# A small weight piece on 24 partitions in 3 steps instead of 16 partitions in 4

## The chip, the cores and the metric

One core of a Trainium2 chip runs the kernel. The metric is device time in microseconds (us) of one execution; lower is better.

## The reference

A decode step for two rows x of width 448: a layer norm, then attention with a cached K and V (16 query heads on 8 kv heads, 4096 positions, head size 256) through w_q and w_o, times the SiLU of a bilinear feed-forward block (width 1792), added to x.

```python
xn = _layernorm(x)                          # x: [2, 1, 448]
q = (xn @ wq).reshape(B, Sq, 16, 256).transpose(0, 2, 1, 3)
p = _softmax(einsum("bhqd,bhkd->bhqk", q, k) * 256 ** -0.5)
s = einsum("bhqk,bhkd->bhqd", p, v).transpose(0, 2, 1, 3).reshape(B, Sq, 4096) @ wo
g = _silu(((xn @ w_gate) * (xn @ w_up)) @ w_down)
return x + s * g
```

All values are float32. K and V alone are 2 x 64 MB; with the weights some 158 MB have to be read once.

## The kernel before

The work is cut into 16 steps i, one for each pair of kv head and batch row. Step i takes K of its pair as k{i} [128, 8192] and V as v{i} [128, 8192]. `scores(i)` (L247) multiplies q with K into PSUM and finds a maximum, `softmax(i)` (L260 to L271) takes the exponential and turns it, `values(i)` (L286) multiplies with V. The main loop runs values(i), then scores(i+1), then softmax(i+1). In between come, after steps 0, 2, 4 and 8, the feed-forward block (`ffn_in`, `ffn_out`), the second half of the queries (`query(1)`) and the first part of the product with w_o (`project`). After the loop comes a tail: scores and values of step 15, the rest of w_o (`project`, and `project_last` at L329, whose weights, wo2, come with the last V), and two VectorE operations and the store (L398 to L400).

What is loaded, and in which order, stands in the list `todo` (filled by `plan`, sent by `issue`). SP issues all loads of K, V and weights into one queue: wq0 (the first half of w_q, at L76), a small piece wqx at L80, k0 (`first`), then `vk` pieces that hold v{i} and k{i+1} together (128 rows of 64 KB), with the other weights between them: wgu, wdq and wo after vk pieces 0, 2 and 8. At the end come last0 (k15 and v14) and last1 (v15 and wo2), the latter in cuts of 4096, 3072, 1024, 1344, 1344, 448, 224 and 224 columns. The K and V buffers are a ring of two, the weights share one slot: SP issues a load when the buffer is free, that is when the reads of its former contents on PE are done. The first four loads wait for nothing.

`query(h)` calls `rows`, which multiplies the 448 rows of w_q's half h with the transposed, normed x. 384 rows are three blocks of 128 (L175). The last 64 rows do not fill 128 partitions. For the second half, and for the feed-forward weights, they are folded: columns of the left half on partitions 0 to 63, of the right half on 64 to 127 (L188). For the first half, wq0 keeps only one of the four column blocks c in folded form on each half (L184, c = 2 and 3); the rows for c = 0 and 1 lie in wqx. It lies on `SIDE` = 16 partitions of 16 KB each: 4 steps times 2 column blocks times 512 columns. Step j of `NK` = 4 multiplies rows 384+16j to 384+16j+15 (L181), once for each column block. The matching pieces of x, xeT, are made by four transposes (L139) and a copy (L140). xeT borrows the start of the tile oT1, which has no other use until the end.

On the host, wqx is built as an array of `SIDE // 4` groups of 5 rows, of which the load reads the first 4: the fifth row is padding that keeps the groups apart in the access pattern. The load is

```python
nc.sync.dma_start(loaded["wqx"][:SIDE], wqx[:, :4])      # L80
```

so 16 partitions on one side stand against 4 groups of 4 rows on the other.

Of the kernel before, what the change touches and what calls it, by code (L numbers as in the profile page):

```python
# [13 lines left out]
B, D = 2, 448  # L14
# [3 lines left out]
W = 32  # L18
DUP = W // 2
NK = 4  # L20
# [6 lines left out]
LATE = 24  # L27
THIRD = [24, 25, 26, 28, 29, 30, 31, 27]
PART = 14 * (D + 512)
SIDE = 16  # L30
EXTRA = 8
EPS = 1e-5


# [5 lines left out]
def gated_decode_block(ctx: ExitStack, tc: tile.TileContext, x, first, vk, last0, last1, wq0, wqx, wdq, wo, wgu, out):  # L40
    nc = tc.nc
# [11 lines left out]
    def bank(name=None):  # L53
        return psum.tile([128, 512], F32, name=name, bufs=1) if name else two()[:, 0]
# [8 lines left out]
    def issue(n=1):  # L63
        for names, src, cuts in todo[:n]:
# [12 lines left out]
            if names == ["wq0"]:  # L77
                at = src.shape[1]
                loaded["wqx"] = t[:, at:at + EXTRA * 512]
                nc.sync.dma_start(loaded["wqx"][:SIDE], wqx[:, :4])  # L80
        del todo[:n]
# [22 lines left out]
    ident = const.tile([128, 128], F32)  # L104
# [18 lines left out]
    xn = e1[:, 1]  # L123
    nc.vector.tensor_scalar(xn[:, :D], xc, rstd, None, op0=OP.mult)
    nc.vector.tensor_scalar(xn[:, D:], xc[:, 384:], rstd, None, op0=OP.mult)
    pt = bank()
# [5 lines left out]


    oT1 = const.tile([128, 3, 2, REP, W], F32)
    xeT = oT1[:SIDE].rearrange("p g d r m -> p (g d r) m")[:, :NK]
    pt = bank()
    for j in range(NK):
        at = 384 + j * SIDE
        nc.tensor.transpose(pt[:SIDE, B * j:B * (j + 1)], xn[:, at:at + SIDE], ident[:B, :B])  # L139
    nc.vector.tensor_copy(xeT.rearrange("p k (b j) -> p k b j", b=B),  # L140
                          pt[:SIDE, :NK * B].rearrange("p (k b) -> p k b", b=B)[:, :, :, None].to_broadcast([SIDE, NK, B, DUP]))

    both = work.tile([128, D], F32, name="h")[:B, :W].rearrange("p (b j) -> p b j", b=B)
    nc.vector.tensor_copy(both, ident[:B, :B, None].to_broadcast([B, B, DUP]))
    pt = bank()
    for c in range(NT):
        nc.tensor.matmul(pt[W * c:W * (c + 1), :SL], both.rearrange("p b j -> p (b j)"), x2[:, c * SL:(c + 1) * SL],
                         start=True, stop=True)
# [18 lines left out]
    def rows(ps, w, n, extra=None):  # L167


        def block(i):  # L170
            return w[:, i * n:(i + 1) * n]

        for k in range(3):
            for c in range(NT):
                nc.tensor.matmul(ps[W * c:W * (c + 1), :n], xnT[:, k, :], block(NT * k + c), start=k == 0, stop=False)  # L175
        if extra is not None:

            for j in range(NK):
                for c in range(2):
                    at = (c * NK + j) * n  # L180
                    nc.tensor.matmul(ps[W * c:W * (c + 1), :n], xeT[:, j, :], extra[:SIDE, at:at + n], start=False, stop=j == NK - 1)  # L181
                    if j == 0:
                        half = slice(64 * c, 64 * (c + 1))
                        nc.tensor.matmul(ps[W * (2 + c):W * (3 + c), :n], xnT[half, 3, :], block(12)[half], start=False, stop=True)  # L184
            return
        for c in range(NT):
            half = slice(0, 64) if c < 2 else slice(64, 128)
            nc.tensor.matmul(ps[W * c:W * (c + 1), :n], xnT[half, 3, :], block(12 + c % 2)[half], start=False, stop=True)  # L188
# [4 lines left out]
    def query(h):  # L193
        ps = bank()
        rows(ps, loaded[f"wq{h}"], 512, None if h else loaded["wqx"])
        for r in range(REP):
            nc.vector.transpose(qT[h][:, :, :, :, r, :].rearrange("p b g d j -> p (g d) b j"),  # L197
                                ps[:, r * 256:(r + 1) * 256])
# [16 lines left out]
    def ffn_in():  # L215
        pp = two()
        for i, w in enumerate(("wg", "wu")):
            rows(pp[:, i], loaded[w], FC)
        g = work.tile([128, FC], F32, name="h")
        nc.scalar.copy(g, pp[:, 0, :FC])  # L220
        h = work.tile([128, FC], F32, name="h")
        nc.vector.tensor_mul(h, pp[:, 1, :FC], g)
        nc.vector.transpose(hT.rearrange("p i m -> p (i m)"), h)
# [34 lines left out]
    def softmax(i, s, m, pT=None):  # L258
        sm = bank("sm")
        nc.tensor.transpose(sm[:1, :128], m[:, 0:1], ident)  # L260
        mx = work.tile([1, NT, W], F32, name="mx", bufs=1)
        nc.vector.tensor_reduce(  # L262
            mx, sm[:1, None, :128].rearrange("p o (c j) -> p o j c", c=NT).to_broadcast([1, NT, W, NT]),
            axis=AX.X, op=OP.max)
        nc.tensor.transpose(sm[:, 128:129], mx.rearrange("p c j -> p (c j)"), one)  # L265
        nc.vector.tensor_scalar(m[:, 1:2], sm[:, 128:129], -1.0 / 16, None, op0=OP.mult)  # L266
        p = work.tile([128, 2, 512], F32, name="p", bufs=1)
        nc.scalar.activation(p, s, AF.Exp, bias=m[:, 1:2], scale=1.0 / 16, accum_out=su[:, place(i):place(i) + 1])  # L268
        if pT is None:
            pT = work.tile([128, 2, 512], F32, name="pT", bufs=1)  # L270
        nc.vector.transpose(pT.rearrange("p h n -> p (h n)"), p.rearrange("p h n -> p (h n)"))  # L271
        return pT
# [66 lines left out]
    p = softmax(0, *ss)  # L339
    for i in range(LAST):  # L340
        g, b = divmod(i, B)
# [9 lines left out]
        p = softmax(i + 1, *ss)  # L351
# [19 lines left out]
    ps = [p]  # L371
# [4 lines left out]
    p = softmax(LAST + 1, *ss, last[:, :1024].rearrange("p (h n) -> p h n", h=2))  # L376
# [75 lines left out]
```

## Time and profile before

| | us |
|---|---|
| median of 3 runs | 376.22 |
| lowest, highest | 376.15, 376.42 |
| the profiled execution | 376.37 |
| its span in the profile | 374.6 |

The span runs from the first to the last instruction of the profile; the 1.8 us beside it are outside of what the profile shows. In the profile, PE is TensorE (PEld its weight loads), DVE is VectorE, ACT ScalarE, SP SyncE, which issues the loads. "L286" is line 286 of the kernel. A chain row gives start, duration and what ran or was waited for. PE does each float32 matmul of 512 columns as two passes, so counts of PE rows are twice those of the code. DMA queue q1 holds the loads that SP issues; q8 and q14, of kind "instruction", are reads of program code.

### The profile page before, as it was taken

How to read it: one execution, taken by the hardware profiler on the slowest of the kernel's cores; microseconds unless marked ns; L12 is line 12 of the kernel's file. 1: busy time of each engine (PE TensorE's matmuls, PEld its weight loads, DVE VectorE, ACT ScalarE, POOL GpSimd, SP SyncE). 2: the span in 40 equal slices, each digit the busy share in tenths (PEclk: the TensorE clock that was granted, in tenths of full speed). 3: DMA queues.
4: the chain of work that ended last, by engine and by line, in shares of the span. 5: the costliest groups of instructions: out<-in, count | busy, mean ns of one | idle time of the engine just before them, and what ended most of it. 6: DMA issues, size and time to landing. Idle time of an engine off the chain costs nothing.

```text
span 374.6 us, 3200 instructions
## 1 busy us (share of the span) xinstructions
PE 203.6 (54%) x1446; PEld 57.3 (15%) x1446; DVE 72.6 (19%) x121; ACT 25.3 (7%) x39; POOL 1.2 (0%) x7
## 2 busy tenths in 40 slices
PE   1796458082734090857372665721819180909785
PEld 0111112020211020212020111200202020202222
DVE  4002130104040003040404041300120312040541
ACT  1000010001020002010101010100010101010120
POOL 1000000000000000000000000000000000000000
PEclk9956598768578577696768596885867687776999
DMA  8999899999999999999999999999999999999994
GB/s 327 432 500 441 374 432 448 448 436 435 419 442 441 441 441 400 422 448 450 420 441 434 443 415 409 457 441 434 450 420 422 441 434 427 436 409 441 413 416 178
DMA packets 4356, 158.78 MB, mean 424 GB/s; under 512 B 614, under 2 KB 1000, under 8 KB 1384
## 3 DMA queue, kind: packets, MB, share of 16 engines
q1 hardware_dynamic: 4340, 158.59, 98.2%
q8 instruction: 11, 0.18, 0.2%
q14 instruction: 1, 0.01, 0.0%
q10 hardware_dynamic: 4, 0.00, 0.0%
HBM read 158.54 MB, written 0.06 MB: 423 GB/s over the span
## 4 chain that ended last, share of the span: by engine, by line
DMA 74%; PE 24%; issue 1%; SPq 0%; DVE 0%
DMA ring<-vk 66%; PE o L286 11%; PE s L247 8%; DMA ring<-last 5%; DMA slot<-wq 3%; PE s L181 2%; PE s L175 1%; PE s L184 1%; PE s L329 0%; SPq L76 0%; PE sm L279 0%; DVE h L398 0%; DVE h L399 0%
## 5 line engine op out<-in xcount | busy, mean ns | idle before, releaser
L286 PE MATMUL o<-ring,pT 128*32 128x512 f32 x480 | 87.3, 893 | 112.4 <-DMA ring<-vk 112.4
L248 DVE TENSOR_REDUCE m<-s 128x1 f32<-128x1024 f32 x16 | 19.6, 1222 | 221.9 <-PE s L247 221.9
L247 PE MATMUL s<-ring,qT 128*32 128x512 f32 x512 | 60.7, 616 | 0.9 <-PE s L181 0.9
L286 PEld LDWEIGHTS o<-ring,pT 128*32 128x32 f32 x480 | 21.7, 155 | 167.8 <-issue 154.2
L268 ACT ACTIVATE p<-s,m 128x1024 f32<-128x1024 f32 x16 | 17.8, 1113 | 293.7 <-DVE m L266 293.7
L247 PEld LDWEIGHTS s<-ring,qT 128*32 128x32 f32 x512 | 17.5, 114 | 42.3 <-issue 39.7
L271 DVE STREAM_TRANSPOSE pT<-p 128x1024 f32<-128x1024 f32 x15 | 18.7, 1245 | 21.2 <-ACT p L268 21.2
L175 PE MATMUL s<-slot,xnT 128*32 128x512 f32 (+1 forms) x96 | 14.1, 733 | 7.3 <-DMA slot<-wq 4.3
L260 PE MATMUL sm<-ident,m 128*1 128x128 f32 x16 | 4.3, 270 | 18.8 <-DVE m L248 18.8
L265 PE MATMUL sm<-one,mx 1*128 1x1 f32 x16 | 3.5, 220 | 14.6 <-DVE mx L262 14.6
L262 DVE TENSOR_REDUCE mx<-sm 1x128 f32<-1x512 f32 x16 | 10.7, 670 | 2.1 <-PE sm L260 2.1
L347 DVE COPY ob<-o 128x512 f32<-128x512 f32 x14 | 9.5, 681 | 0.0
L181 PE MATMUL s<-slot,oT 16*32 16x512 f32 x16 | 7.4, 942 | 0.0
L320 PE MATMUL wide<-slot,oT 128*32 128x448 f32 x48 | 6.6, 699 | 0.6 <-DVE oT L312 0.6
L229 PE MATMUL s<-slot,hT 128*32 128x448 f32 x28 | 4.7, 786 | 3.4 <-DMA slot<-wdq 3.4
L260 PEld LDWEIGHTS sm<-ident,m 128*1 128x1 f32 x16 | 1.3, 79 | 33.0 <-DVE m L248 32.4
L175 PEld LDWEIGHTS s<-slot,xnT 128*32 128x32 f32 x96 | 3.6, 134 | 15.2 <-issue 15.2
L295 PE MATMUL cb<-ob,add_blocks 128*32 128x64 f32 (+2 forms) x64 | 4.3, 384 | 2.4 <-DVE ob L347 1.6
L197 DVE STREAM_TRANSPOSE qT<-s 128x256 f32<-128x256 f32 x4 | 1.6, 428 | 19.4 <-PE s L181 18.4
L265 PEld LDWEIGHTS sm<-one,mx 1*128 1x128 f32 x16 | 2.2, 136 | 17.6 <-DVE mx L262 17.6
L268 ACT ACT_TABLE_LOAD x2 | 2.6, 1283 | 27.4 <-DVE m L266 25.2
L286 PE MATMUL wide<-ring,slot 128*32 128x512 f32 x32 | 4.1, 597 | 0.0
(68 smaller groups left out, 46.8 us busy)
## 6 DMA issues: line engine op xcount, KB each, us to landing
ring<-last SPq DMA_DIRECT2D x2, 4096.0 KB, 24.1
slot<-wdq SPq DMA_DIRECT2D x1, 6720.0 KB
slot<-wgu SPq DMA_DIRECT2D x1, 6272.0 KB, 30.6
slot<-wo SPq DMA_DIRECT2D x1, 5376.0 KB, 41.9
ring<-first SPq DMA_DIRECT2D x1, 4096.0 KB, 21.0
slot<-wq SPq DMA_DIRECT2D x1, 3328.0 KB, 10.7
ring<-last SPq DMA_DIRECT2D x1, 2048.0 KB, 14.1
ring<-last SPq DMA_DIRECT2D x1, 1536.0 KB
```

The source lines that it names most:

```text
L175: nc.tensor.matmul(ps[W * c:W * (c + 1), :n], xnT[:, k, :], block(NT * k + c), start=k == 0, stop=False)
L181: nc.tensor.matmul(ps[W * c:W * (c + 1), :n], xeT[:, j, :], extra[:SIDE, at:at + n], start=False, stop=j == NK - 1)
L247: nc.tensor.matmul(s[W * c:W * (c + 1), h, :], q[:, d], k[:, h, d, c, :], start=d == 0, stop=d == 1)
L248: nc.vector.tensor_reduce(m[:, 0:1], s, axis=AX.XY, op=OP.max)
L260: nc.tensor.transpose(sm[:1, :128], m[:, 0:1], ident)
L262: nc.vector.tensor_reduce(mx, sm[:1, None, :128].rearrange("p o (c j) -> p o j c", c=NT).to_broadcast([1, NT, W, NT]), axis=AX.X, op=OP.max)
L265: nc.tensor.transpose(sm[:, 128:129], mx.rearrange("p c j -> p (c j)"), one)
L268: nc.scalar.activation(p, s, AF.Exp, bias=m[:, 1:2], scale=1.0 / 16, accum_out=su[:, place(i):place(i) + 1])
L271: nc.vector.transpose(pT.rearrange("p h n -> p (h n)"), p.rearrange("p h n -> p (h n)"))
L286: nc.tensor.matmul(o[W * t:W * (t + 1), :], pT[:, h, at:at + 2 * W:2], loaded[f"v{i}"][:, e * 512:(e + 1) * 512], start=e < NT, stop=e >= ...
L320: nc.tensor.matmul(wide[W * t:W * (t + 1), :D], heads(oT, i, first), loaded["wo"][:, i * D:(i + 1) * D], start=i < NT, stop=i >= LATE - NT)
L347: nc.vector.tensor_copy(ob[:, place(i) % 8], o)
```

## The change

wqx is laid on 24 partitions instead of 16, in 3 steps of 24, 24 and 16 rows instead of 4 steps of 16, each partition holding 12 KB instead of 16 KB. The load reads 6 groups of 4 rows instead of 4 groups of 4. The last 8 partitions of the third step are zeros, which are loaded but not used. In all wqx grows from 256 KB to 288 KB. Three transposes instead of four make xeT, two copies instead of one move it (24 and 16 partitions), and the multiplication takes 6 matmuls instead of 8. Nothing else of the program changes, nor the order of the loads.

```diff
-SIDE = 16
-EXTRA = 8
+SIDE = 24
+NS = 3
+EXTRA = 2 * NS
...
-    for j in range(NK):
-        at = 384 + j * SIDE
-        nc.tensor.transpose(pt[:SIDE, B * j:B * (j + 1)], xn[:, at:at + SIDE], ident[:B, :B])
-    nc.vector.tensor_copy(xeT.rearrange("p k (b j) -> p k b j", b=B),
-                          pt[:SIDE, :NK * B].rearrange("p (k b) -> p k b", b=B)[:, :, :, None].to_broadcast([SIDE, NK, B, DUP]))
+    for j in range(NS):
+        lo, hi = 384 + j * SIDE, min(384 + (j + 1) * SIDE, D)
+        nc.tensor.transpose(pt[:hi - lo, B * j:B * (j + 1)], xn[:, lo:hi], ident[:B, :B])
+    for n, lo, hi in ((SIDE, 0, NS - 1), (64 - SIDE * (NS - 1), NS - 1, NS)):
+        nc.vector.tensor_copy(xeT[:n, lo:hi].rearrange("p k (b j) -> p k b j", b=B),
+                              pt[:n, lo * B:hi * B].rearrange("p (k b) -> p k b", b=B)[:, :, :, None].to_broadcast([n, hi - lo, B, DUP]))
...
-            for j in range(NK):
+            for j in range(NS):
+                n_rows = min(SIDE, 64 - j * SIDE)
                 for c in range(2):
-                    at = (c * NK + j) * n
-                    nc.tensor.matmul(ps[W * c:W * (c + 1), :n], xeT[:, j, :], extra[:SIDE, at:at + n], start=False, stop=j == NK - 1)
+                    at = (c * NS + j) * n
+                    nc.tensor.matmul(ps[W * c:W * (c + 1), :n], xeT[:n_rows, j, :], extra[:n_rows, at:at + n],
+                                     start=False, stop=j == NS - 1)
...
     wqx = np.zeros((SIDE // 4, 5, EXTRA * 512), np.float32)
-    ends = wq0[:64, 12 * 512:].reshape(NK, SIDE // 4, 4, 2, 512).transpose(1, 2, 3, 0, 4)
+    ends = np.zeros((NS * SIDE, 2, 512), np.float32)
+    ends[:64] = wq0[:64, 12 * 512:].reshape(64, 2, 512)
+    ends = ends.reshape(NS, SIDE // 4, 4, 2, 512).transpose(1, 2, 3, 0, 4)
```

More of the change, by code (lines that the diff above doesn't have):

```diff
@@ L134, in gated_decode_block @@
     oT1 = const.tile([128, 3, 2, REP, W], F32)
-    xeT = oT1[:SIDE].rearrange("p g d r m -> p (g d r) m")[:, :NK]
+    xeT = oT1[:SIDE].rearrange("p g d r m -> p (g d r) m")[:, :NS]
     pt = bank()
-    for j in range(NK):
-        at = 384 + j * SIDE
-        nc.tensor.transpose(pt[:SIDE, B * j:B * (j + 1)], xn[:, at:at + SIDE], ident[:B, :B])
-    nc.vector.tensor_copy(xeT.rearrange("p k (b j) -> p k b j", b=B),
-                          pt[:SIDE, :NK * B].rearrange("p (k b) -> p k b", b=B)[:, :, :, None].to_broadcast([SIDE, NK, B, DUP]))
+    for j in range(NS):
[4 more added lines that the diff above has]
+                              pt[:n, lo * B:hi * B].rearrange("p (k b) -> p k b", b=B)[:, :, :, None].to_broadcast([n, hi - lo, B, DUP]))
     both = work.tile([128, D], F32, name="h")[:B, :W].rearrange("p (b j) -> p b j", b=B)
```

## The prediction

> **What bounds the kernel now.** I read the page from the top: engines, then the DMA lines, then the queues.
>
> ```profile
> PE 203.6 (54%) x1446; PEld 57.3 (15%) x1446; DVE 72.6 (19%) x121; ACT 25.3 (7%) x39; POOL 1.2 (0%) x7
> ...
> DMA  8999899999999999999999999999999999999994
> ...
> DMA packets 4356, 158.78 MB, mean 424 GB/s; under 512 B 614, under 2 KB 1000, under 8 KB 1384
> ## 3 DMA queue, kind: packets, MB, share of 16 engines
> q1 hardware_dynamic: 4340, 158.59, 98.2%
> q8 instruction: 11, 0.18, 0.2%
> q14 instruction: 1, 0.01, 0.0%
> ```
>
> The loads (q1) keep 16 DMA engines busy 98.2% of the span; PE, the busiest compute engine, 54%. So the time is set by bytes, and more exactly by the DMA engine that is through last. The next view is the chain that ended last, in order of time (start, us, what).
>
> ```profile
> 0.74 10.70 DMA slot<-wq
> 11.44 0.14 issue
> 11.57 4.91 PE s L175 x24
> ...
> 21.23 5.28 PE s L181 x12
> 26.51 0.91 issue
> 27.42 6.41 PE s L247 x32
> 33.83 0.02 issue
> 33.84 42.61 DMA ring<-vk
> ...
> 307.95 29.68 DMA ring<-vk
> 337.63 0.14 issue
> 337.77 6.50 PE o L286 x32
> ...
> 349.55 20.43 DMA ring<-last
> 369.98 0.14 issue
> 370.12 1.45 PE s L329 x48
> ```
>
> From 33.84 on, each stage starts with a landing. Two landings matter: the last vk piece, seen at 337.63 (307.95+29.68), which starts the tail of PE work, and a piece of wo2 seen at 369.98, for which L329 sits idle before its second part:
>
> ```profile
> PE s L329 <- DMA ring<-last: 0.5, 1, 0.5
> ```
>
> **How wqx sits on the DMA engines.** SP issues all that it can, then waits: two rows of its timeline, one of its waits.
>
> ```profile
> 1.18 0.78 SPq L80 DMA_DIRECT2D slot<-wqx  x1
> 2.47 0.50 SPq L76 DMA_DIRECT2D ring<-vk  x1
> ```
>
> ```profile
> SPq L76 <- DMA slot<-wqx: 10.4, 1, 10.4
> ```
>
> SP was free at 2.47+0.50=2.97 and saw wqx land 10.4 later, at 13.4: 1.9 after wq (11.44), though wqx is only 256 KB behind wq's 3328 KB. The DMA view of short windows says why. A DMA closes with a 4-byte packet on each engine that it used. The windows 10.1 to 11.2, 11.2 to 13.1, 19.8 to 20.9 and 22.4 to 22.8, one row each:
>
> ```profile
> DMA packets 37, 0.55 MB, mean 501 GB/s; under 512 B 16, under 2 KB 16, under 8 KB 16
> ```
>
> ```profile
> DMA packets 37, 0.95 MB, mean 500 GB/s; under 512 B 4, under 2 KB 4, under 8 KB 4
> ```
>
> ```profile
> DMA packets 28, 0.92 MB, mean 834 GB/s; under 512 B 12, under 2 KB 12, under 8 KB 12
> ```
>
> ```profile
> DMA packets 16, 0.79 MB, mean 1966 GB/s; under 512 B 4, under 2 KB 4, under 8 KB 4
> ```
>
> "Under 512 B" counts the closing packets: wq closes on 16 engines, wqx on 4; k0 then closes on 12 engines first and on 4 about 2.4 us later. Wqx lies on four engines, which stay behind: SP queues the next DMAs early, so no engine ever waits for the others.
>
> The trace's packet records (which no view lists one by one) let each engine's queue be followed, since a packet starts 4 ns before the one ahead of it ends. I did that for all 16, from wq to the end. A 16 KB packet takes 611 ns, a 12 KB one (the piece 4096 to 7168 of last1) 460, a 64 KB one 2418. Closing packet of the last vk piece, and of wo2's last piece, us:
>
> ```
> engines                           last vk piece     wo2, last piece
> 4, nothing extra                  333.9 to 334.2    367.46 to 367.80
> 6, one q8 fetch                   335.3 to 336.1    368.96 to 369.65
> 2, two q8 fetches                 336.5 and 335.7*  370.10 and 370.24
> 3, wqx                            336.28 to 336.51  369.85 to 370.07
> 1, wqx and the one q14 packet     337.30            370.86
> (* its second fetch came later, at 355.8)
> ```
>
> Two windows confirm the last row: 336.6 to 337.4, then 370.3 to 370.9.
>
> ```profile
> DMA packets 9, 0.26 MB, mean 328 GB/s; under 512 B 1, under 2 KB 1, under 8 KB 1
> ```
>
> ```profile
> DMA packets 16, 0.01 MB, mean 21 GB/s; under 512 B 2, under 2 KB 16, under 8 KB 16
> ```
>
> One engine alone closes the last vk piece; one alone still works from 370.3 on (two closing packets, 21 GB/s; a busy engine's share of 424 is 26.5). It is a wqx engine that was also held up 0.8 us by the q14 packet at 145.1. **The kernel ends when that engine does**, plus what PE does after.
>
> **The change, part by part.**
>
> *The load.* Before: 4 engines x 4 rows x 16 KB. After: 24 partitions against 6 outer groups, so by the same pattern (16 partitions against 4 groups gave 4) 6 engines x 4 rows x 12 KB. Packets start 4 ns early, so a wqx engine carried 4 x (611-4) = 2.43 us and will carry 4 x (460-4) = 1.82: **0.60 us less on each of the four old engines**, the late one among them. Check from the page's mean: 16 KB less on an engine at 26.5 GB/s is 0.62. Two more engines each get 1.82 us that they did not have.
>
> How the engines are chosen, no row names. The Trainium skill ("DMA: Bandwidth & Descriptors", "Why a DMA increments its semaphore by 16 and not by 1") says that a DMA runs on the largest number up to 16 that divides both sides' slowest dimension, and on the lowest-numbered engines; the four closing packets of wqx agree with the number, and by it the new pair would be the fifth and sixth engine.
>
> *Where the 0.60 goes.* Late engine: last vk piece 337.30 to 336.70; next is the two-fetch engine, 336.53, so the whole 0.60 counts. At the end: 370.86 to 370.26; next the other two-fetch engine, 370.24. Again 0.60, and no more than 0.62. If the new pair had nothing extra, they reach 334.2+1.82=336.1 and 367.8+1.82=369.6, below both: no cost.
>
> *The tail of PE.* Chain 337.77 to 369.65 is PE, DVE and ACT work. It starts 0.60 earlier, but the granted clock is half there at first (windows of 3 us; PEclk is third from the end):
>
> ```profile
> 338.00:341.00 3.00, 3.00 (x16) 0.68 (x12) 0.00 (x0) 0.00 (x0) 0.00 (x0) 0.50 0.91 393
> 341.00:344.00 3.00, 3.00 (x20) 0.81 (x16) 0.00 (x0) 0.00 (x0) 0.00 (x0) 0.57 1.09 470
> 344.00:347.00 3.00, 3.00 (x32) 0.94 (x28) 0.00 (x0) 0.00 (x0) 0.00 (x0) 1.00 0.94 404
> ```
>
> If the clock rises at the same moment as before, 0.60 us of half-speed work is worth 0.30. Then PE is ready for L329's second part 0.30 to 0.60 before 369.65, at 369.05 to 369.35. The wo2 piece would be seen 0.60 before 369.98, at 369.38, plus the 0.14 issue: 369.52. So it is still DMA that starts it, and the 0.60 survives. If PE gained nothing at all, it would start at 369.65: 0.47 of 0.60 is kept.
>
> *PE at the start.* L181 has 6 matmuls instead of 8, L139 3 transposes instead of 4.
>
> ```profile
> L181 PE MATMUL s<-slot,oT 16*32 16x512 f32 x16 | 7.4, 942 | 0.0
> L139 PE MATMUL s<-ident,pT 2*16 2x2 f32 x4 | 0.2, 159 | 0.0
> L140 DVE COPY oT<-s 16x128 f32<-16x128 f32 x1 | 0.3, 270 | 0.0
> ```
>
> The 16 rows are 8 matmuls of two passes, paced about 0.47 a pass by 7.4/16. Four passes fewer save 4 x 0.47 = 1.9 us before scores(0). It is worth nothing: vk0 is not there yet, and the timeline has L286 waiting for it (in brackets):
>
> ```profile
> 26.53 0.34 SPq L76 DMA_DIRECT2D slot<-wgu  x1
> ...
> 42.46 3.59 PE L286 MATMUL o<-ring,pT 128*32 128x512 f32 x13 [6.07 <-DMA ring<-vk]
> ```
>
> The 1.9 us only lengthens that 6.07. SP's next DMA (wgu, behind L181) goes out at about 24.6 instead of 26.53; by the packet records vk0 keeps the engines busy to 39.2 at least, so nothing gains. The DVE copy becomes two, +0.27 us, while PE waits for wq until 11.57: hidden; without that cover 0.27 us. No wait is added: PE and SP wait for wqx at the same two places. Between 0 and 1.9 for PE's early part I take 0, since a DMA wait of 6.07 stands behind it.
>
> Sum: **-0.60 us**. Profiled execution: 376.37-0.60=375.77. It ran 0.15 above the median, so against the median 376.22-0.60 = **375.62**, -0.16%. A measurement tells about 0.2% (0.75 us) from no change.
>
> **The rivals.**
>
> 1. *The new pair already carries instruction fetches (slower).* In time order the first eight q8 fetches go to eight different engines, the ninth, tenth and eleventh to the first three again: a ring of eight. None was on a wqx engine; four others had none. So the two new engines come from twelve, of which eight are in the ring. With one fetch, 335.3 to 336.1 plus 1.82 gives 337.1 to 337.9 against 337.30, and 368.96 to 369.65 plus 1.82 gives 370.8 to 371.5 against 370.86: -0.1 to +0.6 us (376.1 to 376.8). With two, 336.53+1.82=338.35 or 370.24+1.82=372.06: +1.05 to +1.2 (377.3 to 377.4). It decides from the point where a new engine's own extra exceeds 337.30-334.2-1.82 = 1.3 us, about one fetch. For it: eight of twelve. Against: the sixteen fall into eight engines of the ring and eight others, and all four of wqx are among the others; if those eight are one block that wqx fills from one end, the next two are in it too. A ring in the middle would not leave them free.
>
> 2. *Bytes count, not the busiest engine.* The load grows by 32 KB; at the mean of 424 GB/s that is +0.08 us: 376.3. The Trainium skill (same page, "Anatomy of one DMA") fits a DMA issued from GpSimd as a fixed time plus its bytes over one rate, which by its 436 GB/s would also be an estimate of +0.08. Against it: the closing packets of k0, four of them 2.4 us late, and one engine alone at the end.
>
> 3. *No gain, another end.* Start-up differs between executions, so two-fetch engines or PE's tail can be last before the late engine is: 0 to -0.3 us, 375.9 to 376.2.
>
> 4. *The DMA does not run on six.* On three engines, 8 rows each, 8 x 0.456 = 3.65 instead of 2.43: +1.2 (377.4); on two, 12 rows, +3.0 (379.3). On sixteen it cannot be even: 24 rows over 16. Against: the four of before.
>
> **How the numbers follow.** Forecast 0.56 (375.4 to 375.9), rival 1 0.28 (0.19 with one fetch, 0.09 with two), rival 2 0.03, rival 3 0.08, rival 4 0.05. The range 375.3 to 376.9 holds the forecast, rivals 2 and 3 and the one-fetch part: 0.86 less their edges. Two fetches and rival 4 are left out. Faster by over 0.2% needs under 375.47, the lower edge of the forecast: 0.10. Slower needs over 376.97: two fetches, rival 4 and a little of one fetch: 0.17. Same: 0.73.
>
> **What would show it.** The window that holds wqx's end has 6 closing packets, earlier (wqx seen near 12.8 instead of 13.4); k0 closes on 10 engines, then on 6 about 1.8 us later; the last vk piece is seen near 337.0, L329's second part starts near 369.5, the span is about 374.0. L181 shows 12 passes. Wrong if k0's late group is not six, if the last vk piece is seen at 337.5 or later (rival 1), or if it is seen earlier and L329 is not (PE's tail).

## The result, and the profile after

The changed kernel takes 376.47 us (median of 19 runs, 376.23 to 377.84), the kernel before 376.26 (19 runs, 376.15 to 376.68): ratio 1.0013, 95% interval 1.0007 to 1.0019. It is a little slower, where 0.60 us less was forecast. The times fall into two clusters: 13 runs from 376.23 to 376.77 (median 376.45), and 6 from 377.53 to 377.84. The kernel before has only one; none of its 69 runs beside the experiments is above 377.13. That 376.47 lies within the 375.3 to 376.9 of the prediction is owed to the rivals for which the range was widened, not to the forecast.

The profiled execution (376.46, span 374.7) is of the lower cluster. The page's DMA lines:

```profile
DMA packets 4366, 158.82 MB, mean 424 GB/s; under 512 B 616, under 2 KB 1002, under 8 KB 1386
## 3 DMA queue, kind: packets, MB, share of 16 engines
q1 hardware_dynamic: 4350, 158.62, 98.2%
q8 instruction: 11, 0.18, 0.2%
q14 instruction: 1, 0.01, 0.0%
```

The load is 10 packets more than before: two more engines, 4 rows and a closing packet each. The share of q1 is what it was. The chain that ended last:

```profile
307.72 29.97 DMA ring<-vk
337.69 0.14 issue
337.83 6.17 PE o L290 x32
...
349.28 20.77 DMA ring<-last
370.06 0.14 issue
370.19 1.09 PE s L333 x40
```

The last vk piece is seen at 337.69 (337.63 before), the wo2 piece at 370.06 (369.98 before). Nothing of the 0.60 us has arrived at either place, and the sign that the prediction named for its first rival, the last vk piece seen at 337.5 or later, is there. PE's early part did become shorter. First the rows of L184, then from the timeline SP's issue of wgu and the first values:

```profile
L184 PE MATMUL s<-slot,oT 24*32 24x512 f32 x8 | 3.1, 600 | 0.0
L184 PE MATMUL s<-slot,oT 16*32 16x512 f32 x4 | 1.0, 588 | 0.0
```

```profile
22.07 0.33 SPq L77 DMA_DIRECT2D slot<-wgu  x1
...
42.24 3.64 PE L290 MATMUL o<-ring,pT 128*32 128x512 f32 x16 [10.09 <-DMA ring<-vk]
```

Twelve passes instead of 16, and wgu goes out at 22.07 instead of 26.53, more than the 1.9 us foreseen, because L184's passes also took a mean of 600 ns or less instead of 942. From 20 to 22 us PE's granted clock was 0.50 before and is 1.00 now: most of these passes now run before the clock falls. It ends as a longer wait for vk0, 10.09 us instead of 6.07: worth nothing, as forecast.

The closing packets of k0, in the windows 20.0 to 21.1 and 21.6 to 22.5, and those of the last vk piece in 336.95 to 337.4:

```profile
DMA packets 26, 0.85 MB, mean 775 GB/s; under 512 B 10, under 2 KB 10, under 8 KB 10
```

```profile
DMA packets 13, 0.46 MB, mean 510 GB/s; under 512 B 6, under 2 KB 6, under 8 KB 6
```

```profile
DMA packets 5, 0.13 MB, mean 291 GB/s; under 512 B 1, under 2 KB 1, under 8 KB 1
```

Ten engines close k0 first, six about 1.8 us later: the load is on six engines with the forecast size. But one engine alone is again late with the last vk piece, at 337.31. Following the queues as for the kernel before:

```
engines                              last vk piece     wo2, last piece
4, wqx only                          335.82 to 336.32  369.39 to 369.88
1, wqx and the q14 packet            336.50            370.06
1, wqx and one q8 fetch (at 244.1)   337.31            370.87
2, two q8 fetches, no wqx            336.90, 335.54*   370.47, 370.52
5, one q8 fetch, no wqx              335.37 to 336.28  368.93 to 369.85
3, nothing extra                     334.10 to 334.39  367.66 to 367.96
(* its second fetch came later, at 355.5)
```

The late engine of before is indeed better off: wqx and q14 now end at 370.06 instead of 370.86. In its place stands an engine with wqx and an instruction fetch, at 337.31 and 370.87, where the old late engine stood at 337.30 and 370.86.

### The profile page after: what moved, and what is told of

Read it like the earlier page. It is cut to its first block, busy times and chain, and to the rows that moved or that the text cites. A ratio compares the mean times of both kernels' runs of the same rounds, so it can differ in the third digit from the quotient of the medians.

```text
span 374.7 us, 3191 instructions
## 1 busy us (share of the span) xinstructions
PE 195.7 (52%) x1441; PEld 56.4 (15%) x1441; DVE 72.6 (19%) x122; ACT 25.3 (7%) x39; POOL 1.3 (0%) x7
## 4 chain that ended last, share of the span: by engine, by line
DMA 77%; PE 21%; issue 0%; DVE 0%; SPq 0%
DMA ring<-vk 68%; PE o L290 10%; PE s L251 8%; DMA ring<-last 6%; DMA slot<-wq 3%; PE s L177 1%; PE s L184 1%; PE s L188 1%; PE s L333 0%; SPq L77 0%; DVE qT L201 0%; PE sm L283 0%; DVE h L402 0%; DVE h L403 0%
## 5 line engine op out<-in xcount | busy, mean ns | idle before, releaser
L290 PE MATMUL o<-ring,pT 128*32 128x512 f32 x480 | 80.4, 831 | 118.2 <-DMA ring<-vk 118.2
L290 PEld LDWEIGHTS o<-ring,pT 128*32 128x32 f32 x480 | 20.5, 147 | 169.8 <-issue 151.5
L299 PE MATMUL cb<-ob,add_blocks 128*32 128x64 f32 (+2 forms) x64 | 6.0, 499 | 2.4 <-DVE ob L351 1.6
L184 PE MATMUL s<-slot,oT 24*32 24x512 f32 (+1 forms) x12 | 4.0, 596 | 0.0
```

The costliest lines, as they stand in the source:

```text
L184: nc.tensor.matmul(ps[W * c:W * (c + 1), :n], xeT[:n_rows, j, :], extra[:n_rows, at:at + n], start=False, stop=j == NS - 1)
L290: nc.tensor.matmul(o[W * t:W * (t + 1), :], pT[:, h, at:at + 2 * W:2], loaded[f"v{i}"][:, e * 512:(e + 1) * 512], start=e < NT, stop=e >= ...
L299: nc.tensor.matmul(cb[W * c:W * (c + 1), :n * 64], add_blocks[:, e].rearrange("p r j -> p (r j)"), src[:, :n, e, :, c, :], start=e == 0, s ...
```

## The experiments

**Theory.** One of the two new engines serves instruction fetches. In the packet records a q8 fetch delays its engine by 1.41 to 1.42 us, the q14 packet by 0.84. So with one fetch the new engine carries 1.82 + 1.41 = 3.23 us, by chance as much as the old late engine (2.43 + 0.84 = 3.27); with two it makes the upper cluster. **Rivals.** The 24-partition layout, its bytes or its PE and DVE work cost the time; or a load on more engines does as such; or the fetch on a wqx engine was an accident of one execution.

**Which engine is which (m_after, m_after2, m_after3).** Three small loads of 5, 8 and 12 rows tell by their packets to which group an engine belongs. No record names an engine: "the sixth" is the one that carries wqx and the loads of 8 and 12 rows, but not that of 5.

```diff
                 nc.sync.dma_start(loaded["wqx"][:SIDE], wqx[:, :4])
+                for j, k in enumerate((5, 8, 12)):
+                    lo = at + EXTRA * 512 + 64 * j
+                    nc.sync.dma_start(t[:k, lo:lo + 24 + 16 * j], mark[:k, :24 + 16 * j])
...
```

> The changed kernel plus three marker loads in SP's queue right behind wqx (5 rows of 96 B, 8 rows of 160 B, 12 rows of 224 B), so that each DMA engine's queue shows by the packets it holds to which of the groups 1 to 5, 6, 7 to 8, 9 to 12, 13 to 16 it belongs. Nothing of the computation changes. Theory (one of the two engines that wqx newly uses is in the ring of eight that serves the instruction fetches, and it ends last): six engines carry wqx; exactly one of the fifth and sixth carries 1 or 2 q8 fetches; the ring's first engine in time is not the same one as in the changed kernel's profile, since the ring goes on from where the last execution stopped. Rival (the fetch on a wqx engine was an accident of that one execution, fetches go anywhere): fetches on engines of the first four too, or on neither of the two. Time near 376.5, or 377.7 if that engine takes two fetches.

Measured: 378.13. The chain and the window 371.2 to 372.3:

```profile
348.35 23.07 DMA ring<-last
371.42 0.14 issue
371.55 1.42 PE s L336 x48
```

```profile
DMA packets 25, 0.04 MB, mean 36 GB/s; under 512 B 3, under 2 KB 24, under 8 KB 24
```

PE waits for the wo2 piece until 371.42, 1.4 us later than in the changed kernel's profile, and a single engine works alone to 372.23 (36 GB/s with the q8 packet of another engine in it). That engine is the sixth, with two fetches.

> The kernel with markers once more, in another execution. Theory: the fetches are on the same engines as in the first look (the sixth, one of 7 and 8, three of 9 to 12, three of 13 to 16), in the same order around the ring but not with the same engine first, except by a chance of one in eight; the sixth takes one fetch, and the time is near 376.5, unless it stands first or second. Rival (the ring starts at the same engine in every execution and the two clusters of times come from something else): the sixth engine takes the 2nd and the 10th fetch again, and the time is 378.1 again or 376.5 with the same fetches.

Measured: 378.10, the sixth engine again with the 2nd and 10th fetch. That was the rival's result: the same start in both executions. So the kernel was run in more executions.

> The kernel with markers, now in many executions. Both looks at it had the sixth engine as the second of the ring, with two fetches and 378.1; the changed kernel's profile had its late wqx engine as the seventh. Theory (the ring's start differs between executions): as for the changed kernel, most times near 376.5 and about a quarter near 378, two clusters. Rival (the start is set by the program, so that this program always has the sixth engine second): all times near 378.1.

Measured: 376.97 (11 runs): 8 from 376.60 to 377.24, 3 from 377.98 to 378.10. Two clusters of one program, so the start is not set by the program. Both clusters lie 0.3 to 0.4 us above those of the changed kernel, and the 378.13 of m_after above the 376.5 or 377.7 that were expected of it. The marker loads are the only difference; where they cost this was not followed. This time the profile is of the lower cluster:

```profile
349.59 20.56 DMA ring<-last
370.15 0.14 issue
370.28 1.08 PE s L336 x40
```

Fetches (us) by group of engines, from the packet records, without the eleventh, which comes after 371 us:

```
engines    m_after (378.13)                 m_after3 (376.97)
1 to 5     none                             none
6          80.3 and 355.4                   263.6
7, 8       106.8                            288.0
9 to 12    155.3; 176.4; 217.6              47.2 and 326.1; 80.9 and 356.1; 104.9
13 to 16   47.2 and 326.1; 264.3; 289.0     154.7; 176.7; 215.3
```

Both columns are the same ring, entered at different places: the sixth engine, one of 7 and 8, three of 9 to 12, three of 13 to 16, and round again. (In m_after3 the engines of the first and the fifth fetch run within 2 ns of each other up to the first; the records don't tell which of them is of 9 to 12 and which of 13 to 16, and the table follows the order of m_after. The sixth, 7 and 8 are clear.) The first two in an execution take two fetches before the end. The sixth is one of these two in 2 of 8 starts; the upper cluster had 6 of 19, here 3 of 11. No execution of the changed kernel's own upper cluster was profiled; the link rests on m_after and m_after2, with two fetches on the sixth, against three profiles with one (after, m_after3, e6x). (In m_after2 the seventh fetch falls on the second engine of 7 and 8 instead of 13 to 16; two queues that run so close together can't be told apart with certainty, and this one is left open.) The q14 packet was on one of the first five each time.

**Five engines with 64 KB (e5g).**

```diff
-SIDE = 24
-NS = 3
+SIDE = 20
+NS = 4
```

> 20 partitions in 4 steps of 16 KB rows, read as 5 groups of 4 rows: five engines with 64 KB each, as much per engine as before. It tells whether the fifth or the sixth engine is the one with fetches. Theory: if it is the sixth, the time is that of before, 376.26, with no second cluster; if it is the fifth, that engine carries 2.43 plus one fetch (1.4) or two, +0.7 us (377.0) in most and +2.0 us (378.3) in about a quarter of the executions. Rival (more engines or more bytes as such cost, 320 KB instead of 256): +0.15 us at 424 GB/s, 376.4.

Measured: 376.46 (11 runs, 376.25 to 376.62), before beside it 376.41: ratio 1.0000 (0.9992 to 1.0009), one cluster. The fifth engine is free, and 320 KB on five engines cost nothing that can be seen. In its profile (376.62) an engine without wqx, with two fetches, closes last, at 371.15; the wqx engines close by 370.70.

**The sixth engine added (e6x).** The changed kernel with rows of 16 KB (a fourth step of zeros that is loaded and not used).

```diff
-NS = 3
+NS = 4
...
-            for j in range(NS):
+            for j in range(3):
...
```

> The changed kernel's work (24 partitions, 3 steps), with rows of 16 KB instead of 12 KB, the last 4 KB of each zeros that are not used: six engines with 64 KB each. Against the five engines with 64 KB of the kernel e5g it adds the sixth engine and nothing else on the other fifteen. Theory (the sixth engine serves instruction fetches, in some executions two): 2.43 plus one fetch of 1.4 makes it last in every execution, about +0.6 us against before (376.9 to 377.1), and 2.43 plus two makes a second cluster near 378.3, in about a quarter. Rival (24 partitions or 12 KB rows are what costs): close to the changed kernel, median 376.5, or to e5g, 376.46, with no cluster above 377.9.

Measured: 377.09 (11 runs): 8 from 376.88 to 377.17, 3 from 378.35 to 378.55; ratio to before 1.0026 (1.0015 to 1.0036). Its profile (377.10) has a wqx engine with one fetch, at 337.95 and 371.52. From e5g to e6x the sixth engine is what is added to a load of 64 KB per engine, and it brings 0.6 us and the second cluster about 2 us above e5g. PE's early part differs too, but in both it ends in a wait of over 9 us for vk0.

**Eight engines with 32 KB (e8g).**

```diff
-SIDE = 24
-NS = 3
+SIDE = 32
+NS = 2
```

> 32 partitions in 2 steps of 8 KB rows, read as 8 groups of 4 rows: eight engines with 32 KB (1.2 us) each. Theory: an engine with wqx and one fetch then carries 2.6 us, less than the 3.3 of the late engine before, so most executions end about 0.5 us earlier (375.7); those in which an engine of the eight takes two fetches carry 3.9 and end about 0.6 us later (376.9): a quarter of them if one of the eight is in the ring, half or more if two or three are. Rival (spreading over more engines costs as such): slower than the changed kernel, over 376.5 throughout.

Measured: 376.66 (11 runs, 376.12 to 377.14), ratio 1.0005 (0.9996 to 1.0014). Not the 375.7 that most executions should have reached, nor over 376.5 throughout, as the rival had it. Its profile (376.92) has two wqx engines with fetches; the one with two closes last, at 371.38. Next comes an engine without wqx, with two fetches, at 370.58, only 0.28 before the last of the kernel before (370.86). The fastest run, 376.12, is likewise only 0.3 under the median of before beside it (376.41): what can be gained here seems to end at that engine.

**The sixth engine left out at 48 KB (e5r60), and all rows on five engines (e5m).** e5r60 has 20 partitions and 3 steps, 60 of the 64 rows, and leaves the other 4 out of the product; e5m adds the last 4 rows by a second load (the last line).

```diff
-SIDE = 24
+SIDE = 20
...
+                nc.sync.dma_start(loaded["wqx"][:4, 2 * NS * 512:], wqy)
```

> Leaves out the last 4 of the 64 rows of w_q's piece, so that 20 partitions in 3 steps of 12 KB hold the rest: five engines with 48 KB each, the load per engine of the changed kernel without the sixth engine. Theory: the -0.60 us that was forecast comes as far as the next engine lets it: the late engine of before ends 0.6 earlier, then the engines with two fetches are last; -0.2 to -0.6 us (375.7 to 376.1), no cluster above 376.9. Rival (the load on the first engines does not set the end, or smaller rows cost): 376.3 to 376.5 as e5g.

Measured: 376.28 (11 runs, 375.99 to 376.94) beside 376.43: ratio 0.9995 (0.9986 to 1.0003). The median is above the expected 375.7 to 376.1. But five of the 11 runs, 375.99 to 376.11, lie under every recorded run of before (lowest 376.14): some executions have part of the gain, others none. Its profile, of the slowest run (376.94), shows what is last: not wqx (370.11 at most) but an engine without wqx, with two fetches, that had also come through wq 1.0 us later than most, at 11.58; it closes at 371.47.

```profile
349.25 21.38 DMA ring<-last
370.63 0.14 issue
370.76 1.37 PE s L333 x48
```

> All 64 rows on the first five engines: 60 as in e5r60, the last 4 by a second load of 4 rows of 4 KB, 0.17 us on each of four engines and one more 4-byte packet. Theory: as e5r60 plus up to 0.17 us, 375.8 to 376.3, a little under before. Rival (a second small load costs more: it writes partitions 0 to 3 from four engines, as the kernel e4g's rows crossed groups of four partitions and its packets took up to 974 ns instead of 460): 376.4 or more.

Measured: 376.43 (11 runs, 376.23 to 376.86) beside 376.43: ratio 0.9999 (0.9990 to 1.0008). Its median is above what was expected and at the rival's 376.4. The rival's reason is not seen: the four 4 KB packets of the second load took 159 ns each, as 4 KB packets elsewhere do. No kernel here beats the one before by more than the measurement tells.

**The 24-partition layout on four engines (e4g).** Meant to keep the layout and take the new engines away.

```diff
-                nc.sync.dma_start(loaded["wqx"][:SIDE], wqx[:, :4])
+                nc.sync.dma_start(loaded["wqx"][:SIDE], wqx[:, :6])
...
-    wqx = np.zeros((SIDE // 4, 5, EXTRA * 512), np.float32)
+    wqx = np.zeros((4, 7, EXTRA * 512), np.float32)
...
```

> The 24-partition layout with its 3 steps, 12 KB rows and two copies, but read as 4 groups of 6 rows, so on four engines with 72 KB each. Theory (which engines carry the load decides): 6 x 0.456 = 2.74 us on each of the four instead of 2.43, +0.3 us against before, median near 376.55, and no second cluster of times near 377.6. Rival (the 24-partition layout itself, its bytes or its PE and DVE work cost the time): like the changed kernel, median 376.47 and about a quarter of the times near 377.6.

Measured: 378.90 (5 runs, 378.76 to 379.19), ratio 1.0067 (1.0055 to 1.0080): neither theory's number, so it says nothing about the layout. The packet records show something else: some 12 KB packets of wqx take 460 ns, others up to 974, and k0's packets up to 2449 ns instead of 1213. An engine now has 6 rows, and its rows cross groups of four partitions.

**72 KB on four engines without crossing (e4w).** The kernel before with rows of 18 KB, the last 2 KB zeros.

```diff
-EXTRA = 8
+EXTRA = 9
...
```

> The kernel before with rows of 18 KB instead of 16 KB, the last 2 KB of each zeros that are not used: four engines with 72 KB each, as in e4g, but each engine's rows stay on four partitions of their own. Theory 1 (e4g was late because its rows of one engine cross groups of four partitions, so that two engines write the same four partitions' port): no such loss here, 4 more times 2 KB at 16 KB per 0.607 us is +0.3 us, 376.6 to 376.8. Theory 2 (72 KB on four engines is itself too much): 378.9 as e4g.

Measured: 376.66 (11 runs, 376.51 to 376.97) beside 376.34, +0.3 us as expected of 4 x 76 ns, one cluster (ratio 1.0006, 0.9997 to 1.0015; the interval holds 1). In its profile the wqx engine with the q14 packet closes at 371.10, 0.24 after the one of before. So 72 KB on four engines explain at most a little of e4g. The rest belongs to what else differs: six rows of 12 KB for an engine, which cross groups of four partitions, instead of four rows of 18 KB, which don't. That it is the crossing, and not the number of rows, is likely but not shown. k0's closing packets in the window 19.8 to 20.9, e4g first, then e4w:

```profile
DMA packets 16, 0.52 MB, mean 477 GB/s; under 512 B 0, under 2 KB 0, under 8 KB 0
```

```profile
DMA packets 28, 0.92 MB, mean 834 GB/s; under 512 B 12, under 2 KB 12, under 8 KB 12
```

In e4w twelve engines have closed k0 by 20.9, as before; in e4g none: the engines that carry no wqx are held up too, by about 1.1 us.

## Why the prediction was wrong, point by point

- **What bounds the kernel: right.** The engine that is last with its queue sets both landings. The sixth engine (e6x) moved the time by what the queues said, +0.6 us; the +0.3 us of 72 KB (e4w) fits too, but is not clear of noise.
- **The load: right.** Six engines, 1.8 us each, two closing groups of 10 and 6. The old late engine went from 370.86 to 370.06. Only wqx's own landing came later than foreseen, 13.1 instead of 12.8, since one of its engines was through wq only at 10.96.
- **PE at the start: right in worth, short in size** (4.5 us earlier instead of 1.9; the wait for vk0 grew by 4.0). The price of 0.47 us a pass mixed passes at full and at half granted clock.
- **"If the new pair had nothing extra": here it failed.** The fifth engine is free, the sixth is in the fetch ring. It was the first rival, given 0.28 against 0.56. Its price with one fetch held: -0.1 to +0.6 us forecast, measured +0.01 us at both closing packets of the profile and +0.19 between the median of the lower cluster and that of before. With two it was too low: 377.3 to 377.4 forecast, 377.53 to 377.84 measured. It added wqx to the two-fetch engines of one execution, and the sixth in m_after, with its markers, ends later, at 372.23 instead of 372.06. What the argument lacked: the four free engines seen then were read as one block that begins behind the wqx engines. They are the fifth, one of 7 and 8, one of 9 to 12 and one of 13 to 16.
- **That a rival is one case or the other: incomplete.** The prediction asked whether the new engine has one fetch or two. It has one in some executions and two in others, since the ring does not start at the same engine each time.
- **The size of 0.60: too large even without the sixth engine.** e5r60 takes it away and leaves out work besides, and is within 0.9986 to 1.0003 of before, which does not hold the forecast -0.16%. The working took the start phases of one execution as given, where the next engine stood 0.62 behind the late one. Rival 3 had it: an engine with two fetches that also starts late, as in e5r60's profile, ends last and does not care for wqx.

The Trainium skill's rule that a DMA runs on the largest number of engines up to 16 that divides the slowest dimension of both sides, and on the lowest-numbered ("DMA: Bandwidth & Descriptors", "Why a DMA increments its semaphore by 16 and not by 1"), agrees with the runs here as far as they show it: 4, 5, 6 and 8 groups closed on as many engines, and the engines of 5, 6, 8 and 12 rows or groups are nested. That they are the lowest-numbered, no row shows.

## What to carry to other kernels

Where DMA is busy throughout, look at the single engine that ends last, not at the bytes: count what each of the 16 carries beyond its equal share, instruction fetches included. Before a small load is given one more engine, find out what else that engine serves, and in more than one execution; the next-late engine limits what can be gained, and it is not the same in each execution. A median may hide two clusters; list the single times.

## What the runs showed of the hardware

- The instruction fetches of this program (q8, 11 packets of 16 KB) go round eight DMA engines: the sixth, one of 7 and 8, three of 9 to 12, three of 13 to 16; none fell on the first five (m_after, m_after3). A fetch holds up its engine's queue by 1.41 to 1.42 us (seven traces, before and after among them), and the ring's first engine differs between executions of one program (m_after, m_after3).
- A load of six rows of 12 KB for each of four engines, which cross groups of four partitions, had packets of up to 974 ns instead of 460 and held up the loads on other engines too: 378.90 us (e4g) against 376.66 (e4w) for the same 72 KB per engine in four rows. That two engines then write through one port is argued, not shown.
